# Cluster-routed attention and a top-1 expert layer: the first expert product with stationary weights, and the last three token blocks in a conditional region

## The chip, the cores and the metric

The kernel runs on one core of one Trainium2 chip. The metric is the device time of one execution in microseconds. Three runs of the kernel before gave 1033.26, 1034.10 and 1034.23 us; the median is 1034.1.

## The reference, cut to what matters

Two layers follow each other. The first is attention over 4 batches, 8 heads, 768 positions and 64 values a head, in which a query sees only keys that chose the same of 16 centroids. Its output is read as 3072 tokens of 512 values. The second is an expert layer that sends each token to one of 8 experts; all in f32:

```
logits = xn @ en.T / tau                  # 3072 x 8
expert_idx = argmax(logits)               # one expert per token
gate_w = softmax(logits)[expert_idx]
for e in range(8):
    mask = expert_idx == e
    h = maximum(x[mask] @ w1[e], 0)       # 512 -> 1024
    out[mask] = gate_w[mask] * (h @ w2[e])  # 1024 -> 512
```

The inputs are drawn from a fixed seed, so the number of tokens of each expert is fixed too; the kernel finds it on the chip.

## The kernel before, in words

Attention runs first, for 16 pairs of heads, up to about 529 us; its order on TensorE, VectorE and ScalarE is written out by hand. Then a routing part (lines 529 to 626) counts the tokens of each expert, gives each expert as many blocks of 128 tokens as it needs, and works out for each of NBLK = 31 blocks, the largest number that 3072 tokens of 8 experts can need: which expert it has (`eblk`), whether that differs from the expert two blocks earlier (`echg`), the row of each of its tokens for the gather (`gidx`) and for the scatter (`sidx`). `nblk` holds the blocks of each expert, `first` the first block of each. A block, or a place in a block, that no token fills gets an index out of bounds for the scatter, so nothing is written for it; before the change such a block is computed all the same.

The expert stage (lines 629 to 732) loops over the 31 blocks. For block j:

- `fetch` (GpSimd, line 639): an indirect DMA gathers 128 token rows from `x_rows`, with the gate weight as a last column. Three buffers.
- `weights` (SyncE, lines 650 to 661): loads the block's expert number and the change flag into registers, then moves the expert's w1 and w2 (2 MB each) into slot j % 2, only if the flag is set. SyncE works in order, so the w1 of the next block stands behind the w2 of this one, which waits until the slot's last second product is done.
- `turn_x` (line 667): four transposes of 128x128 on TensorE put the tokens' 512 values on partitions; VectorE copies them from one PSUM bank to `xT` (line 669).
- `hidden` (line 677): the first product. The tokens `xT` are the stationary operand and w1 moves, 512 columns at a time. A call of `matmul` on f32 is two instructions in the trace, each with its own weight load, so 8 calls are 16 matmuls. ScalarE applies Relu to each of the two banks (line 684). The result has tokens on partitions.
- `turn_h` (line 693): eight transposes on TensorE put the 1024 hidden values on partitions, and VectorE copies them to `hT` in two pieces (line 694).
- `result` (line 700): the second product, again 16 matmuls of 512 columns, with `hT` stationary and w2 moving; ScalarE multiplies by the gate weight (line 708), and GpSimd scatters the rows to the output (line 709).

In the program the order is: fetch j+2, turn_x and hidden of j+1, then turn_h and result of j, then weights j+2. The expert stage isn't under the hand-written order: a planner puts each engine's instructions into a fixed order when the kernel is built. It goes by the place in the program and by which instruction has its inputs ready by its own estimate of durations, and puts in the waits. So a later step can stand ahead of an earlier one on the same engine.

Of the kernel before, what the change touches and what calls it, by code (L numbers as in the profile page):

```python
# [9 lines left out]
F32 = mybir.dt.float32  # L10
BF16 = mybir.dt.bfloat16
I32 = mybir.dt.int32
ALU = mybir.AluOpType
ACTF = mybir.ActivationFunctionType
AXX = mybir.AxisListType.X
EngineType = mybir.EngineType
PSUM = bass.MemoryType.PSUM

P = 128
# [16 lines left out]
def kernel(  # L36
# [12 lines left out]
    nc = tc.nc  # L49
# [3 lines left out]
    E, DM = moe_expert_emb.shape  # L53
    F = moe_w1.shape[2]
# [4 lines left out]
    NSLOT = N // P  # L59
    NBLK = NSLOT + E - 1  # L60
    KD = DM // P
# [9 lines left out]
    const = ctx.enter_context(tc.tile_pool(name="const", bufs=1))  # L71


    w1s = [const.tile([P, KD, F], F32, name=f"w1s{i}") for i in range(2)]
    w2s = [const.tile([P, KF, DM], F32, name=f"w2s{i}") for i in range(2)]

    ident = const.tile([P, P], F32, name="ident")
# [20 lines left out]
    sidx = const.tile([P, NBLK], I32, name="sidx")  # L98
    eblk = const.tile([1, NBLK], I32, name="eblk")
    echg = const.tile([1, NBLK], I32, name="echg")  # L100


    with ExitStack() as at:
# [9 lines left out]
        def misc():  # L113
            return psM.tile([P, 512], F32, tag="misc", name="misc")
# [72 lines left out]
        bk = misc()  # L187
# [12 lines left out]
        bk = misc()  # L200
# [328 lines left out]
        with tc.tile_pool(name="rt", bufs=1) as rt:  # L529

            def rt_tile(shape, dtype, name):
                return rt.tile(shape, dtype, tag=name, name=name)
# [4 lines left out]
                lhsT=onesb,  # L537
                rhs=cumx.rearrange("p s e -> p (s e)"),
                start=True,
                stop=False,  # L540
# [3 lines left out]
                lhsT=sltb,  # L544
                rhs=eq.rearrange("p s e -> p (s e)"),
                start=False,
                stop=True,
# [8 lines left out]
            nblk = rt_tile([P, E], F32, "nblk")  # L556
            first = rt_tile([P, E], F32, "first")
# [3 lines left out]
            nc.vector.tensor_tensor(ee, bc(nblk, [P, E, E], 1), tri, ALU.mult)  # L561
            nc.vector.tensor_reduce(first, ee, axis=AXX, op=ALU.add)
            nc.vector.tensor_scalar(off, first, float(P), None, ALU.mult)


            cmp = rt_tile([1, NBLK, E], F32, "cmp")
# [40 lines left out]
            for s in range(NSLOT):  # L607
                nc.tensor.matmul(
                    inv,
                    lhsT=oh[:, s],  # L610
                    rhs=rr[:, s].rearrange("p t k -> p (t k)"),
                    start=(s == 0),
                    stop=(s == NSLOT - 1),
# [15 lines left out]
    mop = ctx.enter_context(tc.tile_pool(name="mop", bufs=2))  # L629
    psX = ctx.enter_context(tc.tile_pool(name="psX", bufs=1, space=PSUM))  # L630
    psH = ctx.enter_context(tc.tile_pool(name="psH", bufs=3, space=PSUM))
    psR = ctx.enter_context(tc.tile_pool(name="psR", bufs=2, space=PSUM))
    psY = ctx.enter_context(tc.tile_pool(name="psY", bufs=2, space=PSUM))

    mo = {}

    def fetch(j):
        xin = mop.tile([P, XW], F32, tag="xin", name="xin", bufs=3)
        nc.gpsimd.indirect_dma_start(
            out=xin,  # L640
            out_offset=None,
            in_=x_rows[:],
            in_offset=bass.IndirectOffsetOnAxis(ap=gidx[:, j : j + 1], axis=0),
            bounds_check=N - 1,
            oob_is_err=False,
        )
        mo[j] = {"xin": xin}

    def weights(j):
        e = nc.values_load(eblk[0:1, j : j + 1], engines=(EngineType.SP,), min_val=0, max_val=E - 1)  # L650
        c = nc.values_load(echg[0:1, j : j + 1], engines=(EngineType.SP,), min_val=0, max_val=1)
        nc.sync.dma_start(
            out=w1s[j % 2],
            in_=moe_w1[ds(e, 1)].rearrange("o (c p) f -> p (o c) f", p=P),
            cond=c > 0,
        )
        nc.sync.dma_start(
            out=w2s[j % 2],
            in_=moe_w2[ds(e, 1)].rearrange("o (c p) d -> p (o c) d", p=P),
            cond=c > 0,  # L660
        )

    def turn_x(j):
        d = mo[j]
        bk = psX.tile([P, DM], F32, tag="x_ps", name="x_ps")
        for c in range(KD):
            nc.tensor.transpose(bk[:, P * c : P * c + P], d["xin"][:, P * c : P * c + P], ident)  # L667
        d["xT"] = mop.tile([P, DM], F32, tag="xTm", name="xTm")
        nc.vector.tensor_copy(d["xT"], bk)  # L669

    def hidden(j):
        d = mo[j]
        d["h"] = mop.tile([P, F], F32, tag="h", name="h")
        for f0 in range(0, F, 512):
            bk = psH.tile([P, 512], F32, tag="h_ps", name="h_ps")
            for c in range(KD):
                nc.tensor.matmul(  # L677
                    bk,
                    lhsT=d["xT"][:, P * c : P * c + P],
                    rhs=w1s[j % 2][:, c, f0 : f0 + 512],  # L680
                    start=(c == 0),
                    stop=(c == KD - 1),
                )
            nc.scalar.activation(d["h"][:, f0 : f0 + 512], bk, ACTF.Relu)  # L684

    def turn_h(j):
        d = mo[j]
        d["hT"] = mop.tile([P, F], F32, tag="hT", name="hT")
        for f0 in range(0, F, 512):
            bk = psR.tile([P, 512], F32, tag="r_ps", name="r_ps")  # L690
            for c in range(4):
                c0 = f0 + P * c
                nc.tensor.transpose(bk[:, P * c : P * c + P], d["h"][:, c0 : c0 + P], ident)  # L693
            nc.vector.tensor_copy(d["hT"][:, f0 : f0 + 512], bk)  # L694

    def result(j):
        d = mo.pop(j)
        bk = psY.tile([P, DM], F32, tag="y_ps", name="y_ps")
        for c in range(KF):
            nc.tensor.matmul(  # L700
                bk,
                lhsT=d["hT"][:, P * c : P * c + P],
                rhs=w2s[j % 2][:, c],
                start=(c == 0),
                stop=(c == KF - 1),
            )
        y = mop.tile([P, DM], F32, tag="y", name="y", bufs=3)
        nc.scalar.activation(y, bk, ACTF.Copy, scale=d["xin"][:, DM : DM + 1])  # L708
        nc.gpsimd.indirect_dma_start(  # L709
            out=out[:],  # L710
            out_offset=bass.IndirectOffsetOnAxis(ap=sidx[:, j : j + 1], axis=0),
            in_=y,
            in_offset=None,
            bounds_check=N - 1,
            oob_is_err=False,
        )

    for j in range(2):
        weights(j)
        fetch(j)  # L720
    turn_x(0)
    hidden(0)
    for j in range(NBLK):
        if j + 2 < NBLK:
            fetch(j + 2)
        if j + 1 < NBLK:
            turn_x(j + 1)
            hidden(j + 1)
        turn_h(j)
        result(j)  # L730
        if j + 2 < NBLK:
            weights(j + 2)


# [41 lines left out]
```

## Time and profile before

| | us |
|---|---|
| median of three runs | 1034.1 |
| profiled execution | 1039.25 |
| its span, first to last instruction | 1037.5 |
| TensorE matmuls busy (4675) | 985.3 |
| VectorE busy | 336.5 |
| ScalarE busy | 290.9 |
| GpSimd busy | 163.4 |

All rows come from the one profiled execution, so a sum made from them is set against its 1039.25 us first. TensorE's busy time is the union of its matmuls; weight loads are counted apart, since they can run beside a matmul. The ends of matmuls are modelled, so the pace of a row of matmuls is read from starts: the duration of the row, less that of one, over one less than their number.

### The profile page before, as it was taken

What the parts mean: (1) busy time and instruction counts of PE and PEld (TensorE: products, weight loads), DVE (VectorE), ACT (ScalarE), POOL (GpSimd) and SP (SyncE); (2) the same over time, 40 slices, a digit from 0 to 9 for tenths busy, and PEclk for the clock granted to TensorE, in tenths of its full rate; (3) what the DMA queues carried; (4) which work ended last, traced back from release to release, by engine and by line L of the source; (5) the groups of instructions that cost most, each with busy time, mean ns of one, the idle gap of its engine ahead of it and who ended that gap; (6) DMA issues with size and microseconds to landing.
All of it is one profiled execution on the core that took longest, in us unless ns stands there. A gap on an engine that the chain in (4) does not pass through costs nothing.

```text
span 1037.5 us, 11950 instructions
## 1 busy us (share of the span) xinstructions
PE 985.3 (95%) x4675; PEld 481.1 (46%) x4675; DVE 336.5 (32%) x591; ACT 290.9 (28%) x430; POOL 163.4 (16%) x201
## 2 busy tenths in 40 slices
PE   5999999999999999999947999999999999999996
PEld 2444455444544446444533444444444444444443
DVE  2554455555464454454551101101101110110110
ACT  3444444444444443444310111111011111111110
POOL 3011221112211113110131111101101111110110
PEclk8999999999999999799957999999999999999999
DMA  9612222212231211200011373647466563362100
GB/s 263 221 41 46 47 46 77 47 31 47 46 94 30 46 41 37 77 16 1 2 61 31 107 273 104 220 175 280 141 240 237 208 226 114 112 220 85 40 17 0
DMA packets 106119, 107.54 MB, mean 104 GB/s; under 512 B 77445, under 2 KB 77445, under 8 KB 105552
## 3 DMA queue, kind: packets, MB, share of 16 engines
q1 hardware_dynamic: 100928, 92.30, 28.5%
q0 software_dynamic: 4960, 14.44, 3.8%
q8 instruction: 37, 0.61, 0.3%
q14 instruction: 18, 0.15, 0.0%
q10 hardware_dynamic: 176, 0.05, 0.0%
HBM read 165.48 MB, written 14.43 MB: 173 GB/s over the span
## 4 chain that ended last, share of the span: by engine, by line
PE 45%; issue 30%; DMA 17%; DVE 5%; ACT 2%; POOL 0%; POOLq 0%; ACTq 0%; DVEq 0%
DMA out_dram<-y,sidx 17%; PE s_ps L333 15%; PE o_ps L353 13%; PE misc L390 4%; PE misc L216 3%; PE misc L436 3%; PE misc L426 2%; PE misc L273 1%; PE misc L231 1%; PE misc L398 1%; DVE oh L261 1%; DVE xr L404 1%; PE misc L244 1%; DVE pm L260 1%; DVE acc L372 1%
## 5 line engine op out<-in xcount | busy, mean ns | idle before, releaser
L344 ACT ACTIVATE prob<-s_ps 128x768 f32<-128x768 f32 x192 | 155.2, 810 | 249.0 <-PE s_ps L333 242.5
L677 PE MATMUL h_ps<-w1s,xTm 128*128 128x512 f32 x496 | 223.3, 604 | 0.0
L700 PE MATMUL y_ps<-w2s,hT 128*128 128x512 f32 x496 | 218.7, 593 | 1.2 <-DVE hT L694 1.2
L353 PE MATMUL o_ps<-prob,v 128*64 128x384 f32 x768 | 168.3, 517 | 3.7 <-ACT prob L344 3.6
L333 PE MATMUL s_ps<-qT,kT 64*128 64x384 f32 x768 | 157.7, 489 | 0.0
L700 PEld LDWEIGHTS y_ps<-w2s,hT 128*128 128x128 f32 x496 | 93.9, 190 | 118.6 <-issue 116.7
L669 DVE COPY xTm<-x_ps 128x512 f32<-128x512 f32 x31 | 21.4, 691 | 390.8 <-PE x_ps L667 390.8
L677 PEld LDWEIGHTS h_ps<-w1s,xTm 128*128 128x128 f32 x496 | 93.0, 192 | 110.9 <-issue 106.9
L372 DVE TENSOR_TENSOR acc<-acc,prob 128x768 f32<-128x768 f32 x128 | 125.4, 979 | 17.6 <-ACT prob L344 11.3
L684 ACT ACTIVATE h<-h_ps 128x512 f32<-128x512 f32 x62 | 37.0, 597 | 249.0 <-PE h_ps L677 249.0
L709 POOL DMA_INDIRECT out_dram<-y,sidx x31 | 31.4, 1014 | 411.3 <-ACT y L708 411.3
L708 ACT ACTIVATE y<-y_ps,xin 128x512 f32<-128x512 f32 x31 | 21.3, 688 | 188.1 <-PE y_ps L700 188.1
L333 PEld LDWEIGHTS s_ps<-qT,kT 64*128 64x128 f32 x768 | 70.7, 194 | 0.5 <-issue 0.5
L333 PEld LDWEIGHTS <-kH 64*128 64x128 bf16 x384 | 18.5, 93 | 104.0 <-issue 102.5
L333 PE MATMUL s_ps<-qH,kH 64*128 64x384 bf16 x384 | 65.2, 336 | 0.9 <-ACT kH L281 0.9
L353 PEld LDWEIGHTS o_ps<-prob,v 128*64 128x64 f32 x768 | 38.2, 135 | 54.2 <-issue 37.2
L390 PEld LDWEIGHTS misc<-ones,acc 128*128 128x128 f32 x384 | 45.3, 191 | 17.9 <-issue 15.3
L400 DVE RECIPROCAL den<-misc 128x6 f32<-128x6 f32 x32 | 6.3, 196 | 131.6 <-PE misc L398 131.6
L390 PE MATMUL misc<-ones,acc 128*128 128x1 f32 x384 | 48.0, 252 | 0.4 <-DVE acc L372 0.4
L694 DVE COPY hT<-r_ps 128x512 f32<-128x512 f32 x62 | 39.7, 682 | 26.7 <-PE r_ps L693 26.7
L287 POOL TENSOR_TENSOR vs<-v 128x384 f32<-128x384 f32 x16 | 16.0, 998 | 188.8 <-DMA v<-in_v_dram 158.6
L423 POOL TENSOR_TENSOR junk<-xr 128x512 f32<-128x512 f32 x24 | 29.0, 1216 | 90.2 <-DVE sq L444 50.3
(146 smaller groups left out, 700.1 us busy)
## 6 DMA issues: line engine op xcount, KB each, us to landing
w1s<-in_moe_w_dram SPq DMA_DIRECT2D x33, 2048.0 KB
w2s<-in_moe_w_dram SPq DMA_DIRECT2D x33, 2048.0 KB
x_rows<-xr SPq DMA_DIRECT2D x4, 1539.0 KB
q<-in_q_dram SPq DMA_DIRECT2D x32, 192.0 KB
k<-in_k_dram SPq DMA_DIRECT2D x32, 192.0 KB
v<-in_v_dram SPq DMA_DIRECT2D x32, 192.0 KB
xin<-x_rows,gidx POOLq DMA_INDIRECT x31, 7.0
out_dram<-y,sidx POOLq DMA_INDIRECT x31, 6.9
```

The lines of the kernel that those rows point to most:

```text
L216: nc.tensor.transpose(bk[:, P * j : P * j + P], t[nm][:, NJ // 2 * half + j].rearrange("p h d -> p (h d)"), ident,)
L333: nc.tensor.matmul(s_ps[:, h, 0:HS], lhsT=t[l][rows, P * j : P * j + P], rhs=t[r][rows, HS * hq : HS * hq + HS], start=first, stop=not first,)
L344: nc.scalar.activation(d["prob"], d["s_ps"][:, :, 0:HS], ACTF.Exp)
L353: nc.tensor.matmul(g["o_ps"][D * h : D * h + D, 0:HS], lhsT=ld[n]["v"][:, j, h], rhs=d["prob"][:, h], start=(j == 0), stop=(j == NJ - 1),)
L372: nc.vector.tensor_tensor(g["acc"], g["acc"], d["prob"], ALU.add)
L390: nc.tensor.matmul(bk[:, c0 : c0 + 1], lhsT=d["acc"][:, h, P * u : P * u + P], rhs=ones, start=True, stop=True,)
L436: nc.tensor.matmul(bk[:, 0:E], lhsT=t[j][:, P * c : P * c + P], rhs=embT[:, c], start=(c == 0), stop=(c == KD - 1),)
L677: nc.tensor.matmul(bk, lhsT=d["xT"][:, P * c : P * c + P], rhs=w1s[j % 2][:, c, f0 : f0 + 512], start=(c == 0), stop=(c == KD - 1),)
L684: nc.scalar.activation(d["h"][:, f0 : f0 + 512], bk, ACTF.Relu)
L694: nc.vector.tensor_copy(d["hT"][:, f0 : f0 + 512], bk)
L700: nc.tensor.matmul(bk, lhsT=d["hT"][:, P * c : P * c + P], rhs=w2s[j % 2][:, c], start=(c == 0), stop=(c == KF - 1),)
L709: nc.gpsimd.indirect_dma_start(out=out[:], out_offset=bass.IndirectOffsetOnAxis(ap=sidx[:, j : j + 1], axis=0), in_=y, in_offset=None, bou ...
```

## The change

Three things are changed. The first product has its operands exchanged: a 128x128 piece of w1 is stationary and the 128 tokens move, so the result comes out with hidden values on partitions, Relu writes it to `hT` directly, and `turn_h`, its PSUM banks and its copies are gone. The routing computes the number of used blocks, and every engine loads it into a register. The loop becomes a function over a range of blocks; it is called for blocks 0 to 27 (24 + 8 // 2 = 28 blocks), and for 28 to 30 inside a conditional region that runs if more than 28 are used. No step of the one call is interleaved with steps of the other.

```
+    used = const.tile([1, 1], I32, name="used")
...
+            nc.vector.tensor_tensor(
+                used, first[0:1, E - 1 :], nblk[0:1, E - 1 :], ALU.add
+            )
...
     def hidden(j):
...
+        d["hT"] = mop.tile([P, F], F32, tag="hT", name="hT")
         for f0 in range(0, F, 512):
             bk = psH.tile([P, 512], F32, tag="h_ps", name="h_ps")
-            for c in range(KD):
-                nc.tensor.matmul(
-                    bk,
-                    lhsT=d["xT"][:, P * c : P * c + P],
-                    rhs=w1s[j % 2][:, c, f0 : f0 + 512],
...
-            nc.scalar.activation(d["h"][:, f0 : f0 + 512], bk, ACTF.Relu)
+            for m in range(0, 512, P):
+                for c in range(KD):
+                    nc.tensor.matmul(
+                        bk[:, m : m + P],
+                        lhsT=w1s[j % 2][:, c, f0 + m : f0 + m + P],
+                        rhs=d["xT"][:, P * c : P * c + P],
+                        start=(c == 0),
+                        stop=(c == KD - 1),
+                    )
+            nc.scalar.activation(d["hT"][:, f0 : f0 + 512], bk, ACTF.Relu)
-    def turn_h(j):
...
+    def blocks(j0, j1):
+        for j in range(j0, min(j0 + 2, j1)):
+            weights(j)
+            fetch(j)
+        turn_x(j0)
+        hidden(j0)
+        for j in range(j0, j1):
+            if j + 2 < j1:
+                fetch(j + 2)
+            if j + 1 < j1:
+                turn_x(j + 1)
+                hidden(j + 1)
+            result(j)
+            if j + 2 < j1:
+                weights(j + 2)
+
+    usual = NSLOT + E // 2
+    n_used = nc.values_load(used[0:1, 0:1], min_val=NSLOT, max_val=NBLK)
+    blocks(0, usual)
+    with tc.If(n_used > usual):
+        blocks(usual, NBLK)
```

## Rows read from the trace of the kernel before

**Rows 1.** The page's first part: span, busy time, share, instructions.
```profile
span 1037.5 us, 11950 instructions
PE 985.3 (95%) x4675; PEld 481.1 (46%) x4675; DVE 336.5 (32%) x591; ACT 290.9 (28%) x430; POOL 163.4 (16%) x201
```

**Rows 2.** The page's slices of 25.9 us: busy tenths and granted clock.
```profile
PE   5999999999999999999947999999999999999996
...
PEclk8999999999999999799957999999999999999999
```

**Rows 3.** Busy time by stretch: engines, then clock, DMA share, GB/s.
```profile
701.40:716.20 14.80, 14.80 (x45) 7.24 (x44) 1.89 (x3) 1.88 (x3) 2.04 (x2) 1.00 0.86 319
...
1005.90:1021.10 15.20, 15.20 (x46) 7.35 (x45) 1.89 (x3) 1.88 (x3) 1.02 (x1) 1.00 0.00 0
```

**Rows 4.** Waits from 550 us on: total us, times, longest.
```profile
PE x_ps L667 <- DMA xin<-x_rows,gidx: 5.5, 1, 5.5
PE y_ps L700 <- DVE hT L694: 1.2, 3, 0.5
```

**Rows 5.** Timeline of one block: start us, us, engine, line, what.
```profile
716.58 0.60 PE L667 MATMUL x_ps<-ident,xin 128*128 128x128 f32 x4
...
717.02 1.04 PE L693 MATMUL r_ps<-ident,h 128*128 128x128 f32 x8
717.22 0.69 DVE L669 COPY xTm<-x_ps 128x512 f32<-128x512 f32 x1 [13.33 <-PE x_ps L667]
...
717.83 1.28 DVE L694 COPY hT<-r_ps 128x512 f32<-128x512 f32 x2
717.97 7.13 PE L677 MATMUL h_ps<-w1s,xTm 128*128 128x512 f32 x16
...
724.94 7.03 PE L700 MATMUL y_ps<-w2s,hT 128*128 128x512 f32 x16
...
725.14 0.60 ACT L684 ACTIVATE h<-h_ps 128x512 f32<-128x512 f32 x1 [2.78 <-PE h_ps L677]
...
731.80 0.60 PE L667 MATMUL x_ps<-ident,xin 128*128 128x128 f32 x4
```

**Rows 6.** Timeline of weight loads, attention stage: twelve sums of one column.
```profile
502.19 1.42 PEld L390 LDWEIGHTS misc<-ones,acc 128*128 128x128 f32 x12 [0.55 <-issue]
```

**Rows 7.** Groups of weight loads by line: busy us, mean ns, idle before.
```profile
L700 PEld LDWEIGHTS y_ps<-w2s,hT 128*128 128x128 f32 x496 | 93.9, 190 | 118.6 <-issue 116.7 <-DVE hT L694 1.9
...
L693 PEld LDWEIGHTS r_ps<-ident,h 128*128 128x128 f32 x248 | 28.1, 141 | 1.7 <-issue 1.3 <-ACT h L684 0.4
```

**Rows 8.** Timeline from the routing to the first token transposes.
```profile
535.40 0.17 DVE L563 TENSOR_SCALAR off<-first 128x8 f32<-128x8 f32 x1
...
547.72 1.23 POOL L639 DMA_INDIRECT xin<-x_rows,gidx  x1 [4.03 <-DVE sidx L624]
...
551.44 1.09 PE L667 MATMUL x_ps<-ident,xin 128*128 128x128 f32 x4 [5.48 <-DMA xin<-x_rows,gidx]
```

**Rows 9.** Line 650 on SyncE: ns min/median/max, first and last start.
```profile
L650 SPq TENSOR_LOAD <-eblk x31: 262/269/860, 537.7 to 720.7; - x31
```

**Rows 10.** Timeline of the last block's end.
```profile
1022.38 7.13 PE L700 MATMUL y_ps<-w2s,hT 128*128 128x512 f32 x16 [0.35 <-DVE hT L694]
1029.61 0.69 ACT L708 ACTIVATE y<-y_ps,xin 128x512 f32<-128x512 f32 x1 [7.71 <-PE y_ps L700]
1030.57 0.98 POOL L709 DMA_INDIRECT out_dram<-y,sidx  x1 [7.40 <-ACT y L708]
```

**Rows 11.** Closing drain (ns); landings of the last three scatters, of one before.
```profile
L771 POOLq DRAIN  x3: 40/107/6352, 1030.3 to 1037.2; - x3
...
DMA to landing us min/median/max: 2.1/2.1/2.1
...
DMA to landing us min/median/max: 2.8/2.8/2.8
```

More of the change, by code (lines that the diff above doesn't have):

```diff
@@ L631 @@
     psH = ctx.enter_context(tc.tile_pool(name="psH", bufs=3, space=PSUM))
-    psR = ctx.enter_context(tc.tile_pool(name="psR", bufs=2, space=PSUM))
     psY = ctx.enter_context(tc.tile_pool(name="psY", bufs=2, space=PSUM))
@@ L672, in hidden @@
         d = mo[j]
-        d["h"] = mop.tile([P, F], F32, tag="h", name="h")
+        d["hT"] = mop.tile([P, F], F32, tag="hT", name="hT")
         for f0 in range(0, F, 512):
             bk = psH.tile([P, 512], F32, tag="h_ps", name="h_ps")
-            for c in range(KD):
-                nc.tensor.matmul(
-                    bk,
-                    lhsT=d["xT"][:, P * c : P * c + P],
-                    rhs=w1s[j % 2][:, c, f0 : f0 + 512],
-                    start=(c == 0),
-                    stop=(c == KD - 1),
-                )
-            nc.scalar.activation(d["h"][:, f0 : f0 + 512], bk, ACTF.Relu)
-    def turn_h(j):
[L687 to L694, printed above, removed]
+            for m in range(0, 512, P):
[8 more added lines that the diff above has]
+            nc.scalar.activation(d["hT"][:, f0 : f0 + 512], bk, ACTF.Relu)
     def result(j):
@@ L716, in result @@
         )
[L718 to L732, printed above, removed]
+    def blocks(j0, j1):
[18 more added lines that the diff above has]
+        blocks(usual, NBLK)
 _INS = [
```

## The prediction, made before the change was run

> **What bounds the kernel now.** I read the page's busy shares first: of a span of 1037.5 us, TensorE is busy 985.3 [rows 1]. The slices then show that this holds in both halves, at the full clock from slice 23 to the end [rows 2]. So the expert stage, from about 551 us on, is a chain of TensorE instructions, and its waits decide whether that can be taken as a plain sum. They can: in the whole stage TensorE waited 5.5 us for the first gathered tokens and 1.2 us for the turned hidden rows [rows 4]. ScalarE, VectorE and GpSimd wait for TensorE, not the reverse.
>
> One block in the timeline gives the sum [rows 5]. From 716.58 to 731.80, one period of 15.22 us, TensorE does four things: the token transposes for 0.44 us (to 717.02), the eight transposes of the hidden rows with the rest of a wait for VectorE's token copy for 0.95 (to 717.97), the first product for 6.97 (to 724.94) and the second for 6.86. A call on f32 is two instructions, so each product is 16 matmuls of 512 columns: 16 in 7.03 us, the last 0.59 being pipeline, is 0.429 us each. The first product takes 0.10 more than the second, because its first weight load stands alone in front of it.
>
> **The three last blocks.** The count of used blocks follows from the reference's inputs: the experts get 319, 405, 339, 337, 325, 369, 516 and 462 tokens, in blocks of 128 that is 3+4+3+3+3+3+5+4 = 28. The condition "more than 28" is false, so blocks 28 to 30 are jumped over. The trace bears this out: from 1005.9 to 1021.1 the DMA moves 0 GB/s while TensorE is busy all 15.20 us [rows 3], and the last three scatters all land after 2.1 us, a used one after 2.8 [rows 11]. Removed: 3 x 15.22 = 45.7 us, all on TensorE's path, since nothing else runs beside it that is later. The weights are loaded only where the expert changes, so the skipped blocks save no transfer.
>
> **The transposes and copies.** Eight transposes of 128 columns and VectorE's two copies (1.28 us) go from each of 28 blocks. On TensorE that is the 0.95 us of above, in which also the wait for the token copy lay (the copy takes 0.69 us, starting 0.20 after the eight transposes began). With that cover gone the wait is bare: from 717.02 to 717.97 TensorE would have nothing if the first product stood directly behind the token transposes. What can fill it is the second product of the block before: its input is ready, as ScalarE's Relu ended long before (the row at 725.14 lies under the second product of the earlier block). The planner orders TensorE's work by what is ready, and did just this with the eight transposes, which stand behind the first product in the program and ahead of it in the trace. I take the gap as filled: it costs nothing, the price of no cover being 0.95 us x 28 = 26.6 us.
>
> **The first product.** 16 matmuls of 512 columns become 64 of 128 columns, each with a weight load of its own. The columns streamed stay 8192, so the stream alone is 64 x 0.107 = 6.86 us, as now. What is new is that a load comes every 128 columns, and no row of before shows a plain f32 matmul of this shape. Three rows bound it. The stream alone is 0.107 us a pair. The f32 transposes also load 128x128 weights and stream 128 f32 columns: 8 in 1.04 us, less the 0.27 of the last, over 7, is 0.110 us [rows 5]; but their load shows 141 ns and a plain one 190 [rows 7]. The twelve sums with a moving operand of one column show how fast plain f32 loads can follow each other: 12 in 1.42 us, less 0.19, over 11, is 0.112 us [rows 6]. Load and stream thus take almost the same time and must overlap. That they do is seen in the second product, where matmuls follow at the stream's 0.429 though each has its load. The far end, load and stream one after the other, is 0.112 + 0.107 = 0.219. I take 0.111, between the two nearest rows: 64 x 0.111 + 0.10 = 7.20 us, 0.23 more than now.
>
> The Trainium skill speaks against this: by "TensorE: Matmul & The Clock Gate", under "What overlaps and what doesn't" in Part 3, a weight load overlaps a running matmul only where the row group differs. By that rule every pair here would be serial; the 0.429 of the second product, all rows of the array in use, disagrees. It is a rival below.
>
> A block after is then 0.44 + 7.20 + 6.86 = 14.50 us, 0.72 less; over 28 blocks 20.2 us.
>
> **What is added.** In the routing VectorE gets one small addition, like the 0.17 us operation beside it, on the chain that ends in the gather's indices: 0.2 us [rows 8]. Every engine loads the count into a register; the row for such a load on SyncE is 0.27 us, at most 0.86 [rows 9]. TensorE and ScalarE are idle there; GpSimd sits 4.03 us ahead of the first gather. Only VectorE's own load, if put inside the index chain, delays it: queued behind it are the index operations, and the gather and TensorE wait for those. Between 0 and 1.0 us; I take 0.3. SyncE's load stands ahead of the first weight loads, which are not taken for the first expert anyway.
>
> At the end every engine compares and jumps. The trace has no conditional region. Below, it costs nothing: TensorE is done 8 us before the span's end, and ScalarE, the scatter and GpSimd's closing drain (6.35 us, the longest) lie behind it [rows 10, 11]. Above, one more such drain and a handshake make 8 us. I take 1.5, nearer to nothing, because engines branch on their own registers. By the Trainium skill, "Runtime: NRT & Kernel Launch", "Instruction fetch mechanics", a taken jump out of the fetched window stops an engine for a fetch; no run here shows one. The last scatter now lands 0.7 us later, within that drain in part: +0.4.
>
> The weight transfers have to keep up with a shorter block. Where both matrices are loaded, the DMA is 86% busy at 319 GB/s from 701.4 to 716.2 [rows 3], and the first product that needs them starts at 717.97: 1.8 us spare, 1.0 with a block of 14.50. Still hidden.
>
> Sum: -45.7 - 20.2 + 0.2 + 0.3 + 1.5 + 0.4 = -63.5 us. The profiled execution took 1039.25 us (span 1037.5), 0.5% above the median of 1034.1; the same cut scaled by 0.995 is 63.2, which gives 971 us.
>
> **Rivals.**
> 1. The gap stays bare (13%): the planner puts the first product behind its token copy, and TensorE idles 0.95 us a block. For it: nothing of the transposes' cover is left. Against: the second product is ready. 971 + 26.6 = 998; half filled, 984.
> 2. Loads partly exposed (6%): a pair takes 0.12 to 0.14 us. Each 0.01 costs 28 x 64 x 0.01 = 17.9 us: 987 to 1023. For it: a load lasts 190 ns. Against: loads follow each other at 0.112.
> 3. Slower: the loads are not hidden under streams of 128 columns (5%). At 0.190 a pair, the load's own duration, +142: 1113; at 0.219 serial, +193.5: 1164. It decides from 0.111 + 63.2/1792 = 0.146 us a pair on, above which all of the gain is eaten. For it, the skill's rule; against, the transposes' 0.110 with loads as large.
> 4. The conditional region costs a drain (5%): 971 + 6.5 = 977.
> 5. The region runs after all, because the chip's routing counts 29 blocks (1%): three blocks of 14.50, 1014.
>
> **How the numbers follow.** The forecast has 70%, with its own range 962 to 978: a pair of 0.107 gives 7 us less, one of 0.112 2 us more, the region between -1.5 and +6.5. For 8 in 10 the upper end takes in most of rival 1: 960 to 996. About 0.2% is what a measurement of this kernel tells from no change; only rival 3 is slower, 5%; a pair close to 0.146 would make it the same, 1%; the rest is faster, 94%.
>
> **What would show it.** 28 blocks in the trace, each 14.4 to 14.6 us from token transposes to token transposes; 64 matmuls of 128 columns at 0.110 to 0.112 us from start to start; matmuls of the second product between the token transposes and the first product, and no idle TensorE before it; the transposes of the hidden rows gone; nothing after block 27 but the scatter and the closing. The prediction is wrong if TensorE's idle time on the token copy sums to more than 5 us, if pairs take 0.12 or more, or if the time from the last second product to the end is over 12 us against 8.

## The result, and the profile after

The changed kernel takes 971.35 us (median of four runs, 970.65 to 973.44) against 1033.68 for the kernel before: a ratio of 0.940, interval 0.9384 to 0.9417. The prediction was 971 us. Its sum came out, but terms of it were off in opposite directions, and the two profiled executions must not be compared by their spans.

The page after, its first part and the slices (24.2 us each now):

```profile
span 969.8 us, 13780 instructions
PE 916.4 (94%) x5663; PEld 545.8 (56%) x5663; DVE 296.9 (31%) x527; ACT 285.4 (29%) x421; POOL 157.6 (16%) x195
...
PE   4999999999999999999996499999999999999996
...
PEclk9999999999999999999995599999999999999998
```

TensorE is still the bound, with more instructions in less time than in [rows 1]. The span is 67.7 us shorter, more than the medians' 62.3. The clock row tells why: the 8 in the first slice and the 7 in the seventeenth of [rows 2] are gone. These two answers (stretch, its length, busy time of the engines, then clock, DMA share, GB/s) show that stretch in the kernel before, and in a run of this study whose attention code is that of the kernel after:

```profile
412.50:426.20 13.70, 13.70 (x58) 7.55 (x60) 7.36 (x17) 3.55 (x5) 0.84 (x5) 0.50 0.00 0
```

```profile
412.30:426.00 13.70, 13.70 (x57) 7.58 (x56) 7.36 (x17) 3.44 (x5) 0.80 (x4) 0.50 0.00 0
```

The clock was granted at half (0.50, the level of 1.2 GHz) and TensorE started 58 matmuls in 13.7 us. The kernel after, in the execution profiled, started 105 at the full clock in the like stretch. As the stretch also comes with the code of after, it belongs to the execution and not to the change. What the executions differ by up to the expert stage is read from the first token transposes: they start at 551.44 in [rows 8] and at 547.75 after, 3.7 us earlier. The other traces have the same: the two with the whole stretch start there at 551.35 and 551.39, the others between 544.85 and 547.85. So the stage behind them is compared by itself: from there to the end of the last second product it took 478.1 us [rows 8, 10] and takes 413.5, and from that end to the span's end 8.0 and 8.6. Together 64.0 less. About 0.9 of this is still the clock, an estimate: the stage began at half the clock in both, for 7.86 us before and 6.05 after, and half of the difference is lost.

One block after, in TensorE's timeline (start us, us, engine, line, what):

```profile
924.90 0.60 PE L670 MATMUL x_ps<-ident,xin 128*128 128x128 f32 x4
925.34 1.02 PE L695 MATMUL y_ps<-w2s,hT 128*128 128x512 f32 x2
926.28 7.41 PE L682 MATMUL h_ps<-xTm,w1s 128*128 128x128 f32 x64
933.53 6.17 PE L695 MATMUL y_ps<-w2s,hT 128*128 128x512 f32 x14
939.54 0.60 PE L670 MATMUL x_ps<-ident,xin 128*128 128x128 f32 x4
```

A period is 14.64 us, against 15.22 in [rows 5]. The planner did fill the gap with the second product, but with two matmuls only: they fill 0.86 us from 925.34, and the first product starts 0.94 after it. The 64 pairs: 7.41 less 0.28 of the last, less 0.10 of the first load that stands alone, over 63, is 0.1116 us each. Four early blocks have more filling, and these take 14.45:

```profile
588.15 3.60 PE L695 MATMUL y_ps<-w2s,hT 128*128 128x512 f32 x8
591.58 7.31 PE L682 MATMUL h_ps<-xTm,w1s 128*128 128x128 f32 x64
598.73 3.60 PE L695 MATMUL y_ps<-w2s,hT 128*128 128x512 f32 x8
602.16 0.60 PE L670 MATMUL x_ps<-ident,xin 128*128 128x128 f32 x4
```

Here the product's row is 7.31 and no longer 7.41: the first load too was done under the filling.

The waits of the stage that bear on it (total us, times, longest):

```profile
PEld h_ps L682 <- DVE xTm L672: 15.7, 21, 0.8
...
PE h_ps L682 <- DMA w1s<-in_moe_w_dram: 0.9, 1, 0.9
```

The first is the weight load's, not TensorE's: 21 times the first load waited for the token copy, 0.75 us each, while the two matmuls of the second product still ran. The load of w1 doesn't need the tokens, yet in the trace it is the load that stands behind the wait for them.

The end:

```profile
948.17 13.04 PE L695 MATMUL y_ps<-w2s,hT 128*128 128x512 f32 x30
```

```profile
L733 PEldq COMPARE_BRANCH  x1: 3482/3482/3482, 953.9 to 953.9; - x1
...
L733 ACTq COMPARE_BRANCH  x1: 45/45/45, 961.9 to 961.9; - x1
...
L733 POOLq COMPARE_BRANCH  x1: 45/45/45, 962.6 to 962.6; - x1
L733 POOLq INC_SWDGE_SEM  x1: 1296/1296/1296, 963.0 to 963.0; - x1
```

The columns of the second fence are ns, then the first and last start in us. TensorE's queue reached its branch at 953.9, while its last matmuls ran until 961.2: the 3.48 us of the branch are hidden. GpSimd's come last: its load of the count (0.51 us at 962.0), the branch and 1.30 us of INC_SWDGE_SEM. I take this last one to make good the signals that the skipped region would have given; no run shows what it does. The closing drain comes behind it, 4.64 us long and not 6.35 as in [rows 11], so only a part of these steps adds to the time.

### The profile page after: what moved, and what is told of

Read it like the earlier page. It is cut to its first block, busy times and chain, and to the rows that moved or that the text cites. A ratio compares the mean times of both kernels' runs of the same rounds, so it can differ in the third digit from the quotient of the medians.

```text
span 969.8 us, 13780 instructions
## 1 busy us (share of the span) xinstructions
PE 916.4 (94%) x5663; PEld 545.8 (56%) x5663; DVE 296.9 (31%) x527; ACT 285.4 (29%) x421; POOL 157.6 (16%) x195
## 4 chain that ended last, share of the span: by engine, by line
PE 48%; issue 25%; DMA 19%; DVE 5%; ACT 2%; POOL 1%; POOLq 0%; ACTq 0%; DVEq 0%
DMA out_dram<-y,sidx 19%; PE s_ps L334 16%; PE o_ps L354 14%; PE misc L391 5%; PE misc L217 3%; PE misc L437 3%; PE misc L427 2%; PE misc L274 1%; PE misc L232 1%; PE misc L399 1%; DVE oh L262 1%; PE misc L245 1%; DVE xr L405 1%; DVE pm L261 1%; DVE acc L373 1%
## 5 line engine op out<-in xcount | busy, mean ns | idle before, releaser
L682 PEld LDWEIGHTS h_ps<-xTm,w1s 128*128 128x128 f32 x1792 | 204.5, 193 | 19.9 <-DVE xTm L672 15.7
L682 PE MATMUL h_ps<-xTm,w1s 128*128 128x128 f32 x1792 | 208.6, 278 | 0.9 <-DMA w1s<-in_moe_w_dram 0.9
L695 PE MATMUL y_ps<-w2s,hT 128*128 128x512 f32 x448 | 201.2, 592 | 0.0
L354 PE MATMUL o_ps<-prob,v 128*64 128x384 f32 x768 | 166.3, 512 | 4.7 <-ACT prob L345 4.5
L672 DVE COPY xTm<-x_ps 128x512 f32<-128x512 f32 x28 | 19.4, 691 | 378.4 <-PE x_ps L670 378.4
L695 PEld LDWEIGHTS y_ps<-w2s,hT 128*128 128x128 f32 x448 | 81.0, 190 | 81.3 <-issue 81.3
L689 ACT ACTIVATE hT<-h_ps 128x512 f32<-128x512 f32 x56 | 33.4, 597 | 240.5 <-PE h_ps L682 240.5
L704 POOL DMA_INDIRECT out_dram<-y,sidx x28 | 28.5, 1017 | 353.6 <-ACT y L703 347.7
L703 ACT ACTIVATE y<-y_ps,xin 128x512 f32<-128x512 f32 x28 | 19.2, 688 | 137.8 <-PE y_ps L695 131.6
L255 POOL TENSOR_TENSOR sel<-sel,prefc 128x384 bf16<-128x384 bf16 x16 | 24.3, 1518 | 119.1 <-DVE sel L254 114.0
```

Source lines behind the costliest of these rows:

```text
L354: nc.tensor.matmul(g["o_ps"][D * h : D * h + D, 0:HS], lhsT=ld[n]["v"][:, j, h], rhs=d["prob"][:, h], start=(j == 0), stop=(j == NJ - 1),)
L682: nc.tensor.matmul(bk[:, m : m + P], lhsT=w1s[j % 2][:, c, f0 + m : f0 + m + P], rhs=d["xT"][:, P * c : P * c + P], start=(c == 0), stop=( ...
L689: nc.scalar.activation(d["hT"][:, f0 : f0 + 512], bk, ACTF.Relu)
L695: nc.tensor.matmul(bk, lhsT=d["hT"][:, P * c : P * c + P], rhs=w2s[j % 2][:, c], start=(c == 0), stop=(c == KF - 1),)
L704: nc.gpsimd.indirect_dma_start(out=out[:], out_offset=bass.IndirectOffsetOnAxis(ap=sidx[:, j : j + 1], axis=0), in_=y, in_offset=None, bou ...
```

## The experiments

All ratios are to the kernel before, run beside them.

**The yardstick.** 

> The changed kernel once more, as the yardstick for the others on this chip: 971 us, within 1 us. Where another run is compared, it is compared with this one.

Measured: 971.5 us, ratio 0.9402 (0.9379 to 0.9424).

**The region alone.**

```
     def blocks(j0, j1):
...
+            turn_h(j)
             result(j)
...
+    with tc.If(n_used > usual):
+        blocks(usual, NBLK)
```

> The kernel before with the count and the conditional region alone; the first product and the transposes of the hidden rows stay as they were. Theory (each skipped block was 15.22 us of TensorE's path, the region costs under 1.5): 1033.7 - 45.7 + 0.6 = 988.6 us, within 1.5. Rival (part of the three blocks was hidden, or the region costs a drain): 992 or more.

Measured: 987.97 us, ratio 0.9531 (0.9484 to 0.9578): 46.2 us less. The stage took 431.9 us in the trace, 46.2 less too. The three blocks lay on the path with their whole length.

**The first product alone.**

```
-    with tc.If(n_used > usual):
-        blocks(usual, NBLK)
+    blocks(0, NBLK)
```

> The changed first product for all 31 blocks, no count and no region. Theory (blocks of 14.64 against 15.22 us): 31 x 0.58 = 18.0 us less than before: 1015.7 us, within 2; with the region alone it adds up to the whole cut of 62.3. Rival (the gain comes from somewhere else, for example from the end or the start of the stage): less than 12 us.

Measured: 1012.9 us, ratio 0.9783 (0.9734 to 0.9832): 21.3 us less, 3.3 more than expected. The trace agrees (stage 456.8, 21.3 less). Half of the miss is in the start. From the first token transposes to the fourth block's, the kernel before took 42.8 us (551.44 to 594.22), this run 39.4 (544.85 to 584.25), and most of what is more than 3 x 0.58 there is the clock and not the change. The two stages began at half the clock for 7.86 and for 4.95 us, so some 1.5 us were given back (an estimate, half of the difference):

```profile
551.44:559.30 7.86, 7.08 (x14) 3.58 (x15) 0.69 (x1) 0.00 (x0) 0.12 (x1) 0.50 0.22 57
```

```profile
544.85:549.80 4.95, 4.16 (x19) 3.77 (x20) 0.69 (x1) 0.00 (x0) 0.12 (x1) 0.51 0.29 90
```

The rest: I had taken 0.58 us for each block, but the early blocks gain 0.77, and the kernel before waited three times for the copies of the turned rows [rows 4].

For 28 blocks, the region's run and the yardstick are the fair pair. Both have the region, and both stages start at the same time and run at half the clock until about 554.9. The first and last rows of the stage, the region's run first:

```profile
546.85 1.08 PE L671 MATMUL x_ps<-ident,xin 128*128 128x128 f32 x4 [5.46 <-DMA xin<-x_rows,gidx]
...
971.61 7.13 PE L704 MATMUL y_ps<-w2s,hT 128*128 128x512 f32 x16 [0.35 <-DVE hT L698]
```

```profile
546.86 1.09 PE L670 MATMUL x_ps<-ident,xin 128*128 128x128 f32 x4 [5.50 <-DMA xin<-x_rows,gidx]
...
948.02 13.04 PE L695 MATMUL y_ps<-w2s,hT 128*128 128x512 f32 x30
```

That is 431.9 and 414.2 us: the new first product is worth 17.7. With the region's 46.2, less 0.6 for the longer closing, it makes 63.3, and the trace after shows 64.0, or 63.1 without the clock's 0.9. So the two parts add up to the whole.

**No region, 28 blocks.**

```
-    with tc.If(n_used > usual):
-        blocks(usual, NBLK)
...
-    blocks(0, usual)
+    blocks(0, NSLOT + E // 2)
```

> The changed kernel with the condition, the count and the last three blocks left out altogether: 28 blocks, unconditionally (right only for inputs that use 28). Theory (the engines branch on their own registers, behind work that ends later anyway): the region costs 0 to 1.5 us, so 969.5 to 971. Rival (the jump costs a drain or an instruction fetch on the path that sets the end): 963 to 966.

Measured: 969.6 us, ratio 0.9386 (0.9362 to 0.941). By the medians the region costs 1.9 us, which their intervals don't tell from nothing. The traces do: the last second product ends at 965.0 of a span of 972.5, so 7.5 us to the end, against 8.5 to 8.7 in all eight traces in which the region is skipped.

```profile
956.68 8.32 PE L691 MATMUL y_ps<-w2s,hT 128*128 128x512 f32 x19
```

The region costs 1.1 us, not a drain: the theory holds, and rival 4 of the prediction falls.

**The gap bare.**

```
-    blocks(0, usual)
+    with tc.manual_schedule(engines={EngineType.PE}):
+        blocks(0, usual)
```

> The changed kernel with TensorE's order in the expert stage fixed to that of the program: token transposes of j+1, first product of j+1, second product of j, so that no matmul stands between the transposes and the first product. Theory (the planner's filling with the second product is what saved the gap): a bare wait of 0.95 us a block instead of the 0.08 left now, so 27 x 0.87 = 23.5 us more: 995 us. Rival (the token copy was hidden anyway): 971 us.

Measured: 995.2 us, ratio 0.963 (0.9607 to 0.9654), 23.7 more than the yardstick. The timeline of TensorE and its wait:

```profile
733.81 0.60 PE L670 MATMUL x_ps<-ident,xin 128*128 128x128 f32 x4
735.19 7.41 PE L682 MATMUL h_ps<-xTm,w1s 128*128 128x128 f32 x64 [0.78 <-DVE xTm L672]
742.44 7.03 PE L695 MATMUL y_ps<-w2s,hT 128*128 128x512 f32 x16
749.31 0.60 PE L670 MATMUL x_ps<-ident,xin 128*128 128x128 f32 x4
```

The first product starts 1.38 us after the token transposes, just as in the kernel after; but nothing stands between, and the second product, whole, comes later. The period is 15.50 us. What the removed transposes had covered is worth 0.86 us a block, and the planner's order alone kept it.

**Tokens turned earlier.**

```
+                hidden(j + 1)
+            if j + 3 < j1:
+                weights(j + 3)
+            result(j, 0, KF - FILL)
+            if j + 2 < j1:
+                turn_x(j + 2)
+            result(j, KF - FILL, KF)
+            if j + 2 < j1:
+                weights2(j + 2)
```

FILL is 2 calls, so four matmuls; TensorE's order is the program's, and `weights2` is the move of w2. 

> The changed kernel with TensorE's order written out so that four of the second product's matmuls (1.72 us) stand between the token transposes and the first product instead of two (0.86 us), and with each block's w1 issued ahead of the w2 of the block before, so that SyncE's queue does not hold it back. Theory (0.08 us of wait and the 0.10 us of a first weight load that waits for the token copy are left in each block): 27 x 0.18 = 4.9 us less: 966.5 us, blocks of 14.46. Rival (these 0.18 us are the switch between streams, and no wait): 971 us, blocks of 14.64.

Measured: 967.54 us, ratio 0.936 (0.9341 to 0.9378), the fastest of the kernels here that leave nothing out, 4 us below the yardstick. The period is 14.45 in 25 of 27 blocks:

```profile
731.61 0.60 PE L675 MATMUL x_ps<-ident,xin 128*128 128x128 f32 x4
732.05 1.88 PE L702 MATMUL y_ps<-w2s,hT 128*128 128x512 f32 x4
733.77 7.31 PE L687 MATMUL h_ps<-xTm,w1s 128*128 128x128 f32 x64
740.91 5.32 PE L702 MATMUL y_ps<-w2s,hT 128*128 128x512 f32 x12
746.06 0.60 PE L675 MATMUL x_ps<-ident,xin 128*128 128x128 f32 x4
```

The 0.18 us was wait and an uncovered load, as the theory said. The run changed a second thing, the earlier issue of w1; it shows apart from this, as the one long block of the kernel after (15.64 us) is gone.

**Half of the columns.**

```
-                        bk[:, m : m + P],
+                        bk[:, m : m + P // 2],
...
-                        rhs=d["xT"][:, P * c : P * c + P],
+                        rhs=d["xT"][:, P * c : P * c + P // 2],
```

> The changed kernel, but the first product streams only 64 of each block's 128 tokens (Relu copies each result twice, so the output is that of half the tokens); the number of weight loads stays. Theory A (the load sets the pace of a pair): the pair stays at 0.11 us, the time at 971 within 3. Theory B (the stream sets it, with a fixed addition for each matmul): the pair falls to about 0.06 us, the time by about 28 x 64 x 0.05 = 90 us to 881. Theory C (load and stream partly one after the other): in between, 0.085 us a pair, about 926.

Measured: 1048.8 us in one run, outside all three theories. The pair is as theory A has it: 64 in 7.25 us, less 0.28, over 63, is 0.111.

```profile
710.50 7.25 PE L682 MATMUL h_ps<-xTm,w1s 128*128 128x64 f32 x64
722.13 1.09 PE L670 MATMUL x_ps<-ident,xin 128*128 128x128 f32 x4 [4.38 <-DMA xin<-x_rows,gidx]
723.01 9.39 PE L698 MATMUL y_ps<-w2s,hT 128*128 128x512 f32 x16
```

The 77 us come from elsewhere: with other sizes the planner wrote another order, in which TensorE waited 44.9 us for gathers (14 times, 1.8 to 4.5 us each), and in or just behind 13 of these waits the clock fell to half. The stretch around the wait at 722 (columns as above):

```profile
720.90:727.70 6.80, 5.57 (x10) 2.93 (x11) 0.69 (x1) 0.00 (x0) 0.00 (x0) 0.50 0.66 270
727.70:741.40 13.70, 11.79 (x75) 9.01 (x73) 0.00 (x0) 2.00 (x5) 2.05 (x2) 1.00 0.54 182
```

**Half of the columns, in a fixed order.** The same edit in the kernel that turns tokens earlier. 

> The run with 64 of 128 tokens moved once more, in the written-out order of the run that turns tokens early, so that the planner cannot reorder and TensorE does not wait for gathers (half of the tokens' first product is left out, as there). Theory A (the load sets the pace of a pair): the same as that order with 128 columns, 967.5 within 2 us, pairs of 0.111. Theory B (the stream sets it): about 90 us less. [...]

Measured: 982.4 us, ratio 0.9506 (0.9453 to 0.956). The waits for gathers are gone, and a period is 14.45 us, to the hundredth that of 128 columns:

```profile
730.88 0.60 PE L675 MATMUL x_ps<-ident,xin 128*128 128x128 f32 x4
731.31 1.88 PE L705 MATMUL y_ps<-w2s,hT 128*128 128x512 f32 x4
733.03 7.25 PE L687 MATMUL h_ps<-xTm,w1s 128*128 128x64 f32 x64
740.12 5.37 PE L705 MATMUL y_ps<-w2s,hT 128*128 128x512 f32 x12
745.33 0.60 PE L675 MATMUL x_ps<-ident,xin 128*128 128x128 f32 x4
```

So half the stream changes nothing, and what is left to set the pace is what each pair needs once, the weight load above all. Whether it is the load itself or another fixed part of an f32 pair, no run tells. The issue of a load and a matmul alone can be faster: in the routing of the kernel before, 24 bf16 pairs follow each other at 0.051 us (1.42 less 0.24, over 23), at half the clock:

```profile
544.54 1.42 PE L608 MATMUL misc<-rr,ohr 128*128 128x62 bf16 x24 [10.50 <-DVE rr L602]
```

But the total is 15 us more than expected. It lies at the start of the stage, where the clock stayed at half until 583.4 and not 553.8. The first fence is this run, the second the one with 128 columns:

```profile
548.00:583.40 35.40, 33.83 (x142) 30.46 (x142) 1.38 (x2) 2.63 (x8) 0.00 (x0) 0.50 0.12 40
```

```profile
553.80:583.40 29.60, 28.82 (x202) 23.98 (x202) 1.38 (x2) 4.27 (x7) 2.05 (x2) 1.00 0.25 90
```

29.6 us at half the clock instead of the full one is 14.8 us lost, an estimate from these two rows; the medians differ by 14.8 and the stages in the two traces by 13.6 (423.0 against 409.4). In the first run with 64 columns the clock stayed at half to 571 there. Why it rose so late is open.

**Half of the loads.**

```
-            for m in range(0, 512, P):
+            for m in range(0, 512, 2 * P):
...
-                        bk[:, m : m + P],
+                        bk[:, m : m + 2 * P],
```

> The changed kernel, but the first product has 32 matmuls of 256 columns instead of 64 of 128 in each block: the same columns streamed, half the weight loads (the columns come from two neighbouring 128-wide pieces, so half of the products are left out and others are wrong). Theory A (the load sets the pace at 0.1116 where the stream would need 0.107): the product falls to the stream's 32 x 0.216 = 6.9 us, 0.25 a block, 7 us less in all: 964. Theory B (a fixed addition for each matmul, not the load): about the same, 965. If the pace comes from the columns alone: 971.

Measured: 964.96 us, ratio 0.9326 (0.9271 to 0.938), 6.4 below the kernel after, with periods of 14.40 and 14.21 us: 0.24 less in each, as theories A and B both had it.

```profile
729.01 7.17 PE L682 MATMUL h_ps<-xTm,w1s 128*128 128x256 f32 x32
```

32 in 7.17, less 0.38 and 0.10, over 31, is 0.2158 us: the stream of 256 columns (half of the 0.429), and no load is seen. The runs with 64 columns tell the two apart, for A: there theory B would have made the pair shorter, and it stayed at 0.111.

**The region taken.**

```
-    with tc.If(n_used > usual):
+    with tc.If(n_used > usual - 1):
```

> The changed kernel with the condition set to more than 27, so that the conditional region runs: the same output, and the price of the case that the change keeps out of the way. Rival 5 of the prediction priced it as three blocks of the usual length: 971.4 + 3 x 14.64 = 1015 us. Theory now: no step of the region may start before the branch, and GpSimd's branch stands behind its last scatter, so the first gather, its landing, the token copy and a first product without cover stand bare once more, as at the start of the stage (3.7 us from gather to transposes, 1.4 to the product), and the scatter and register load ahead of it (3 us): 8 us or more on top, 1023 to 1028.

Measured: 1026.5 us, ratio 0.9935 (0.9907 to 0.9963): 55.0 more than the kernel after, three blocks of 14.64 and 11.1 on top.

```profile
960.08 1.05 POOL L642 DMA_INDIRECT xin<-x_rows,gidx  x1 [0.30 <-issue]
...
964.17 1.09 PE L670 MATMUL x_ps<-ident,xin 128*128 128x128 f32 x4 [6.42 <-DMA xin<-x_rows,gidx]
...
966.04 1.11 PE L670 MATMUL x_ps<-ident,xin 128*128 128x128 f32 x4 [0.79 <-DVE xTm L672]
...
968.85 9.29 PE L682 MATMUL h_ps<-xTm,w1s 128*128 128x128 f32 x64
```

The gather can't start before GpSimd has branched, so TensorE stands 6.42 us, turns three blocks one after the other, and runs at half the clock from 962.8 to 973.0. Even with the region taken the kernel isn't slower than before.

## Why the prediction was right

**The bound and the block.** Right. A chain of TensorE instructions, added up from starts in one block, gave the price of a block (14.64 us against 14.50 predicted) and the direction of the change in it (0.58 against 0.72). The prediction's list of waits left out one, 0.8 us for the first block's token copy in the trace of before, which changes nothing in the sum.

**The three blocks.** 45.7 us predicted, 46.2 measured by the region alone (45.5 in its trace, closing included).

**The first product and the transposes.** 20.2 predicted, 17.7 measured: the pair wasn't the reason, the gap was (below). The pair was right to the last digit that counts: 0.111 predicted, 0.1116 measured. So is the reason now: 64 columns are as slow as 128, 256 reach the stream's pace. Loads by themselves follow each other at the 0.112 of [rows 6], and the stream of 128 columns runs beside them. Rivals 2 and 3 fall. So does, for this kernel, what the Trainium skill's "TensorE: Matmul & The Clock Gate" says under "What overlaps and what doesn't", that a load overlaps a running matmul only where the row group differs: with all rows of the array in both, the pair took 0.1116 us, and one after the other would be 0.219.

**The gap.** Here the step was too good. "I take the gap as filled: it costs nothing" holds where four or more matmuls stand in it. In 21 blocks the planner put two, 0.86 us against the 0.94 until the copied tokens are there, and the first load of the product, which by the sum lay bare anyway, stayed so: a block of 14.64, just outside the 14.4 to 14.6 that the prediction named as its sign, where 14.45 was to be had. Rival 1's price was right: 23.7 us measured with the gap bare, where 0.86 of the 0.95 us a block were still covered.

**What is added.** Predicted +2.4 us (0.2 + 0.3 + 1.5 + 0.4), measured about +0.7. The addition in the routing costs 0.05 to 0.2: from the operation ahead of it to the first token transposes it is 16.04 us in [rows 8], and 547.75 - 531.54 = 16.21 after, 16.08 and 16.13 in the region's run and the yardstick.

```profile
531.54 0.17 DVE L564 TENSOR_SCALAR off<-first 128x8 f32<-128x8 f32 x1
531.62 0.14 DVE L565 TENSOR_TENSOR used<-first,nblk 1x1 int32<-1x1 f32 x1
```

VectorE's register load cost nothing, as the planner put all loads but SyncE's in front of the branches (VectorE's at 940.2). The closing grew by 0.6. The region is 1.1 of it; without it the closing was half a microsecond shorter than before, which no run explains. The last scatter does land later, after 2.6 us against 2.1 in [rows 11], but nothing became longer by it. By the Trainium skill's "Runtime: NRT & Kernel Launch", "Instruction fetch mechanics", a taken jump out of the window waits for a fetch. TensorE's branch, over some 500 instructions, took 3.48 us and those of ScalarE and GpSimd, over few, 0.05, which fits; no run shows that it is a fetch, and nothing waited for it.

**The weights.** "Still hidden" is right but for one wait of 0.95 us, at 911.7, in the one block of 15.64 us.

So the sum's terms of the stage were 2.0 us too large a gain (65.9 against 46.2 + 17.7), those around it 1.7 too large a loss. That the median came out to a third of a microsecond is chance; that it came within two is not.

## What to carry to other kernels

Before a product is turned around, read from any row of back-to-back loads how fast they follow each other, and compare it with the stream per load: here 0.112 against 0.107 us, so 128 columns just about hide an f32 load, and 64 don't. Where a step goes that also covered a wait, ask what stands there next, and write the order down if it matters: the same matmuls took 995, 971.5 or 967.5 us by order alone. The region that was jumped over cost about a microsecond at this kernel's end, but taken it started cold, 11 us above its work.

## What the runs showed of the hardware

- The granted clock moved within one execution, at a price of some 15 us in one run. In the first run with 64 columns it stood at half (1.2 GHz) for 6.8 us around a wait of 4.38 us for a gather. In the second it rose to full at 583.4, in the run with 128 columns and the same order at 553.8, though at the full clock the loads of the two follow each other at the same pace.
- At half the clock a pair takes double: 64 in 13.49 us from first to last start in the first product of the second run with 64 columns, 6.98 later.
- One and the same attention code ran with and without a stretch of 13.7 us at half the clock near 412 us. The two profiled executions of before and after differ by 3.7 us ahead of the stage, more than some of the effects studied here, so spans of single profiles don't settle them. The stage by itself does, once the time that it begins at half the clock (4.8 to 8.1 us in the runs with 128 columns or more) is set against it.
